# A decode step of attention beside a gated feed-forward layer: one section with its own semaphores, and a loop on TensorE

## The chip, the cores and the metric

The kernel runs on one core of a Trainium2 chip. The metric is the device time of one execution in microseconds. Three timed executions of the kernel before took 2523.05, 2523.11 and 2523.18 us; the median, 2523.11 us, is the time before. The engines are called as the profile calls them: PE is TensorE (PEld its weight loads), DVE is VectorE, ACT is ScalarE, POOL is GpSimd, and SP is SyncE, whose queue starts nearly all transfers. The data itself is moved by 16 DMA engines.

## What is computed

One token `x` of 512 values goes through two branches. Branch A is attention with 32 heads over a cache of 65,536 keys and values of 128 each; branch B is a gated feed-forward layer. A scalar gate mixes them.

```python
g = sigmoid((x * gate_w).sum(-1, keepdims=True))
q = (x @ wq)                                  # 32 heads of 128
scores = einsum("bhqd,bhkd->bhqk", q, k_cache) * (128 ** -0.5)
p = softmax(scores, axis=-1)
a = einsum("bhqk,bhkd->bhqd", p, v_cache) @ wo  # heads side by side
b = (silu(x @ w_gate) * (x @ w_up)) @ w_down
return g * a + (1 - g) * b
```

The two caches hold 32 x 65536 x 128 bf16 numbers each, 537 MB apiece. All else is small beside them.

## The kernel before

The caches are cut into N = 128 tiles. A tile is 128 keys on each of 128 partitions (NB = 128 keys of 128 numbers, 4 MB), and a head has G = 4 of them. Two tiles make a pair (8 MB), so there are M = 64 pairs, and two pairs to a head. The main loop (L424) is unrolled in Python and takes one pair a step. An even step (`first`) begins a head, an odd step ends it.

SBUF holds two K buffers of a pair each (`take`, `give`, the tiles `K_t`) and one V buffer of a pair (`V_buf`). In a step, DVE multiplies the K tile by the query in place (`products`, L261, 128x16384), halves the 128 products of each key to 16 by three additions in place (L265), and later reduces what TensorE made of them (`fold`, L289). TensorE adds the 16 columns of a key by four matmuls with the identity (`scores`, L274). After a head's last tile come the maximum (`row_max`), the exponentials on ACT (`exponentials`, L308) and their sum (`total`, `weight`). TensorE then multiplies the probabilities of the head before by its V tiles, 32 matmuls a tile (`values`, L330); with V two pairs behind K, step i works on V of pair i - 2. DVE takes the sums of a finished head out of PSUM (`head_copy`, L350 and L361), TensorE turns them into a column (`head_turn`, L367), ACT writes it to `oT` (L397), and at the end `project` (L406) multiplies all heads by `wo`.

The order of the work on each engine is written out by hand in that loop; the framework adds the semaphores. Two things in it matter here. In an odd step TensorE runs `values(2i-4)` ahead of `scores(2i)`; in an even step `scores(2i)` comes first. And the V loads are issued where their buffer comes free: after each half in an even step (`load_v(2i-2)`, `load_v(2i-1, 1)`, two transfers of 4 MB), after both halves in an odd step (`load_v(2i-2)`, one transfer of 8 MB). The K load of pair i + 2 (`load_k(i + 2)`) follows behind `scores(2i+1)`. SP issues all of these in this order, so that V of pair i - 1 and K of pair i + 2 alternate on its queue; both go through line 114. TensorE's program is the longest of all: every matmul of all 64 steps is in it once.

The feed-forward layer and the gate are worked into the first two steps, and the last pair of each cache and `wo` are loaded in smaller pieces at the end, into buffers that have come free.

Of the kernel before, what the change touches and what calls it, by code (L numbers as in the profile page):

```python
# [12 lines left out]

NB = 128
PAIR = 2 * NB
SLOTS = 2

QUAD = 4  # L20
# [5 lines left out]
V_CUTS = {3: (0, 64, NB), 2: (0, 64, NB), 1: (0, 32, 64, 96, 112, NB - TURNED, NB)}  # L26
EARLY = 16
LATE_CUTS = (EARLY, 24, 28, 30, 32)

GROUPED = 28  # L30


@with_exitstack
def kernel(
# [28 lines left out]
    assert Dh == P and G == 4 and NBH == 512 and H * D <= PAIR * Dh  # L63
    scale = float(Dh) ** -0.5

    consts = ctx.enter_context(tc.tile_pool(name="consts", bufs=1))
    ring = ctx.enter_context(tc.tile_pool(name="ring", bufs=1))
    small = ctx.enter_context(tc.tile_pool(name="small", bufs=2))
    psum_s = ctx.enter_context(tc.tile_pool(name="psum_s", bufs=2, space=bass.MemoryType.PSUM))
    psum_o = ctx.enter_context(tc.tile_pool(name="psum_o", bufs=2, space=bass.MemoryType.PSUM))  # L70
    psum_a = ctx.enter_context(tc.tile_pool(name="psum_a", bufs=1, space=bass.MemoryType.PSUM))
    psum_m = ctx.enter_context(tc.tile_pool(name="psum_m", bufs=2, space=bass.MemoryType.PSUM))

    ctx.enter_context(tc.manual_schedule())


    free = list(range(SLOTS))
    held = {}

    def take(name):  # L80
        slot = free.pop(0)
        held[name] = slot
        return ring.tile(
            [P, PAIR * Dh], bf16, name=name.split(".")[0], tag=f"slot{slot}"
        )

    def give(name):
        free.append(held.pop(name))


# [3 lines left out]
    consts.tile([P, 96], bf16, name="fill")  # L94
    xT = consts.tile([P, KT], bf16, name="xT")
    gwT = consts.tile([P, KT], bf16, name="gwT")
    with nc.allow_non_contiguous_dma(reason="small"):
        nc.scalar.dma_start(out=xT, in_=A_x[0, 0, :].rearrange("(p t) -> p t", t=KT))
        nc.scalar.dma_start(out=gwT, in_=gate_w.rearrange("(p t) -> p t", t=KT))

    nc.sync.dma_start(  # L101
        out=V_buf[:, : KT * H * Dh], in_=A_wq.rearrange("(p t) f -> p (t f)", t=KT)
    )
    wq_sb = V_buf[:, : KT * H * Dh].rearrange("p (t f) -> p t f", t=KT)

    K_tiles, V_tiles, S_tiles, F_tiles, P_tiles, O_tiles, q_tiles = {}, {}, {}, {}, {}, {}, {}


    def load(view, cache, m, cuts, start=0):
        h, g = divmod(m, MH)  # L110
        rows = cache[0, h, g * PAIR * P : (g + 1) * PAIR * P, :]
        src = rows.rearrange("(p j) d -> p j d", j=PAIR)
        for a, b in zip(cuts[:-1], cuts[1:]):
            nc.sync.dma_start(out=view[:, a:b, :], in_=src[:, start + a : start + b, :])

    def load_k(m):
        view = take(f"K_t.{m}").rearrange("p (j d) -> p j d", d=Dh)
        load(view, A_k_cache, m, (0, NB, PAIR) if m in (0, M - 1) else (0, PAIR))
        for i in range(2):
            K_tiles[2 * m + i] = view[:, i * NB : (i + 1) * NB, :]  # L120

    def load_v(n, half=0, spare=None):
        if n % G == 0 and spare is None:
            view = V_buf.rearrange("p (j d) -> p j d", d=Dh)
            V_tiles[n], V_tiles[n + 1] = view[:, :NB, :], view[:, NB:, :]
            load(view, A_v_cache, n // 2, (0, PAIR))
        else:
            view = V_buf if spare is None else spare
            view = view[:, half * NB * Dh : (half + 1) * NB * Dh]
            V_tiles[n] = view = view.rearrange("p (j d) -> p j d", d=Dh)  # L130
            load(view, A_v_cache, n // 2, V_CUTS.get(N - n, (0, NB)), n % 2 * NB)

    load_k(0)
    load_k(1)

    ident_f = consts.tile([P, P], f32, name="ident_f")
    make_identity(nc, ident_f[:])
    ident_b = consts.tile([P, P], bf16, name="ident_b")
    nc.scalar.activation(out=ident_b, in_=ident_f, func=ACT.Copy)
    ones_f = consts.tile([P, P], f32, name="ones_f")  # L140
    nc.vector.memset(ones_f, 1.0)

    ones_b = consts.tile([P, P], bf16, name="ones_b")
    nc.vector.memset(ones_b, 1.0)

    qT = consts.tile([P, H], f32, name="qT")
    rowsum = consts.tile([P, H], f32, name="rowsum")
    oT = consts.tile([P, H], bf16, name="oT")
    gval = consts.tile([P, 1], f32, name="gval")
    rg = consts.tile([P, H], f32, name="rg")  # L150
    HD = D // 2
    a_ps = [psum_a.tile([1, HD], f32, name=f"a{i}_ps") for i in range(2)]

    def queries():
        q_ps = psum_m.tile([P, H], f32, name="q_ps", tag="misc")
        for h in range(H):
            for t in range(KT):
                nc.tensor.matmul(
                    q_ps[:, h : h + 1],
                    lhsT=wq_sb[:, t, h * Dh : (h + 1) * Dh],  # L160
                    rhs=xT[:, t : t + 1],
                    start=(t == 0),
                    stop=(t == KT - 1),
                )
        nc.scalar.activation(out=qT, in_=q_ps, func=ACT.Copy)

    def query(h):
        diag = small.tile([P, P], bf16, name="q_diag")
        nc.scalar.activation(out=diag, in_=ident_f, func=ACT.Copy, scale=qT[:, h : h + 1])  # L169
        qb_ps = psum_m.tile([P, P], f32, name="qb_ps", tag="misc")  # L170
        nc.tensor.matmul(qb_ps, lhsT=ones_b, rhs=diag, start=True, stop=True)  # L171
        q_tiles[h] = small.tile([P, P], bf16, name="q_sb")
        nc.scalar.activation(out=q_tiles[h], in_=qb_ps, func=ACT.Copy)  # L173

    def load_wo(tile, cuts):
        t = tile[:, : H * D].rearrange("p (h n) -> p h n", n=D)
        runs = t.rearrange("p (g j) n -> p g (j n)", j=QUAD)
        rows = A_wo.rearrange("(h p) n -> p h n", p=P)
        row_runs = A_wo.rearrange("(g p j) n -> p g (j n)", p=P, j=QUAD)
        for a, b in zip(cuts[:-1], cuts[1:]):  # L180
            if b <= GROUPED:
                a, b = a // QUAD, b // QUAD
                nc.sync.dma_start(out=runs[:, a:b, :], in_=row_runs[:, a:b, :])
            else:
                nc.sync.dma_start(out=t[:, a:b, :], in_=rows[:, a:b, :])
        return t

    def feed_forward_in():
        gu_ps = psum_m.tile([P, 2 * FT], f32, name="gu_ps", tag="misc")
        for w in range(2):  # L190
            cols = wgu_sb[:, w].rearrange("p t (m c) -> p t c m", c=FT)
            for ft in range(FT):
                for t in range(KT):
                    nc.tensor.matmul(
                        gu_ps[:, w * FT + ft : w * FT + ft + 1],
                        lhsT=cols[:, t, ft, :],
                        rhs=xT[:, t : t + 1],
                        start=(t == 0),
                        stop=(t == KT - 1),
                    )  # L200
        gu_sb = consts.tile([P, 2 * FT], f32, name="gu_sb")
        nc.scalar.activation(out=gu_sb, in_=gu_ps, func=ACT.Copy)
        eg = consts.tile([P, FT], f32, name="eg")
        nc.scalar.activation(out=eg, in_=gu_sb[:, :FT], func=ACT.Exp, scale=-1.0)
        return gu_sb, eg

    def gate_sum():
        xg = consts.tile([P, KT], f32, name="xg")
        nc.vector.tensor_tensor(out=xg, in0=xT, in1=gwT, op=ALU.mult)
        xs = consts.tile([P, 1], f32, name="xs")  # L210
        nc.vector.tensor_reduce(out=xs, in_=xg, axis=AXIS.X, op=ALU.add)
        return xs

    def gate_exp(xs):
        g_ps = psum_m.tile([P, 1], f32, name="g_ps", tag="misc")
        nc.tensor.matmul(g_ps, lhsT=ones_f, rhs=xs, start=True, stop=True)
        eg2 = consts.tile([P, 1], f32, name="eg2")
        nc.scalar.activation(out=eg2, in_=g_ps, func=ACT.Exp, scale=-1.0)
        return eg2

    def gate_value(eg2):
        nc.vector.tensor_scalar_add(eg2, eg2, 1.0)
        nc.vector.reciprocal(gval, eg2)
        rest = consts.tile([1, 1], f32, name="rest")
        nc.vector.tensor_scalar(
            out=rest, in0=gval[0:1, :], scalar1=-1.0, scalar2=1.0, op0=ALU.mult, op1=ALU.add
        )
        return rest
# [41 lines left out]
    def scores(n):  # L270
# [11 lines left out]
        if n % 2:  # L282
            give(f"K_t.{n // 2}")
# [276 lines left out]
```

## Time and profile before

| What | Value |
|---|---|
| median of three timed executions | 2523.11 us |
| the profiled execution's own time | 2523.22 us |
| its span, first to last instruction | 2521.4 us |
| read from HBM | 1087.64 MB |
| busy: DVE / PE / PEld / ACT / POOL | 2260.4 / 1274.2 / 490.8 / 100.5 / 0.7 us |
| instructions on PE, as the trace records them | 5232 matmuls and 5232 weight loads |
| L261, product of a K tile | x128, 8685 ns each |
| L330, matmul of V | x4032, 409 ns recorded, 986.4 us together |
| L350 and L361, a head's sums | x31 each, 671 ns and 1020 ns |

A profile is one execution of the program, recorded instruction by instruction. Its span is a little shorter than its time, by 1.8 us here, which lie ahead of the first and behind the last recorded instruction. A group's "idle before" is the time its engine stood still just before its instructions, with the event that ended the wait. The chain of waits follows back from the last instruction to what released it, step by step. A queue's packets are what the DMA engines moved for it; the queue that is marked "instruction" brings the programs of the engines themselves.

### The profile page before, as it was taken

Reading aid. Unit: us, or ns where it says so; the run is one execution under the profiler, and the core shown is the slowest. Engines: PE = TensorE matmul, PEld = TensorE weight load, DVE = VectorE, ACT = ScalarE, POOL = GpSimd, SP = SyncE. Lnnn points to the kernel's source line nnn. Section 1 sums busy time; section 2 is a strip of 40 time slices with the busy share of each in tenths; the row PEclk is TensorE's granted clock in tenths of the full one; section 3 lists DMA queues with packets and bytes.
Section 4 is the critical chain, followed back from the end, with each engine's and each line's share of the span. In section 5 each row is a group of like instructions: output and inputs, shape, how many; then the busy total and the mean of one; then the engine's idle time right before and its main releaser. Section 6 shows DMA issues by size and latency. Waiting matters only on the chain.

```text
span 2521.4 us, 12044 instructions
## 1 busy us (share of the span) xinstructions
PE 1274.2 (51%) x5232; PEld 490.8 (19%) x5232; DVE 2260.4 (90%) x830; ACT 100.5 (4%) x317; POOL 0.7 (0%) x6
## 2 busy tenths in 40 slices
PE   3544654536535455444455453554545544446548
PEld 2211211212212122111122121221211211112213
DVE  5899999989999989899999898999998989999993
ACT  0000000000000000000000000000000000000000
POOL 0000000000000000000000000000000000000000
PEclk8767767767767677676777776776767767677779
DMA  9999999999999999999999999999999999999998
GB/s 415 436 434 433 436 435 430 436 434 433 433 430 436 435 432 432 435 433 442 432 433 432 430 435 434 437 432 433 432 436 432 435 437 429 437 432 432 433 432 374
DMA packets 26888, 1088.42 MB, mean 432 GB/s; under 512 B 3154, under 2 KB 3667, under 8 KB 4947
## 3 DMA queue, kind: packets, MB, share of 16 engines
q1 hardware_dynamic: 26546, 1087.65, 99.8%
q8 instruction: 41, 0.67, 0.1%
q14 instruction: 13, 0.10, 0.0%
q10 hardware_dynamic: 288, 0.00, 0.0%
HBM read 1087.64 MB, written 0.00 MB: 431 GB/s over the span
## 4 chain that ended last, share of the span: by engine, by line
DMA 51%; DVE 46%; PE 2%; issue 1%; another core or an unknown queue 0%; DVEq 0%; SPq 0%; ACT 0%
DMA K_t<-in_A_k_cache_dram 49%; DVE K_t L261 23%; DVE K_t L265 20%; PE S_ps L274 2%; DVE o_row L361 1%; DMA V_buf<-in_A_v_cache_dram 1%; DVE S_sb L289 1%; DVE O_sb L350 1%; DMA wo_late<-in_A_wo_dram 1%; PE O_ps L330 0%; DVE top L304 0%; PE a_ps L406 0%; DVEq L261 0%; SPq L101 0%
## 5 line engine op out<-in xcount | busy, mean ns | idle before, releaser
L261 DVE TENSOR_TENSOR K_t<-K_t,q_sb 128x16384 bf16<-128x16384 bf16 x128 | 1111.7, 8685 | 142.8 <-DMA K_t<-in_A_k_cache_dram 142.8
L330 PE MATMUL O_ps<-V_buf,P_sb 128*4 128x512 bf16 x4032 | 986.4, 409 | 361.4 <-DMA V_buf<-in_A_v_cache_dram 360.5
L265 DVE TENSOR_TENSOR K_t<-K_t 128x2048 bf16<-128x2048 bf16 (+1 forms) x372 | 996.0, 2677 | 8.3
L274 PE MATMUL S_ps<-K_t,ident_b 128*128 128x512 bf16 x576 | 208.3, 503 | 807.2 <-DVE K_t L265 806.8
L330 PEld LDWEIGHTS <-P_sb 128*4 128x4 bf16 x4094 | 364.9, 90 | 980.3 <-issue 534.3
L274 PEld LDWEIGHTS <-ident_b 128*128 128x128 bf16 x576 | 62.4, 113 | 899.4 <-issue 877.3
L289 DVE TENSOR_REDUCE S_sb<-S_ps 128x128 f32<-128x512 f32 x128 | 87.4, 683 | 65.9 <-PE S_ps L274 65.9
L397 ACT ACTIVATE oT<-oh_ps,rg 32x1 bf16<-32x1 f32 x112 | 28.6, 255 | 696.9 <-PE oh_ps L367 695.9
L299 PE MATMUL mT_ps<-diag,ones_f 128*128 128x128 f32 x64 | 24.8, 490 | 60.2 <-ACT diag L297 60.1
L173 ACT ACTIVATE q_sb<-qb_ps 128x128 bf16<-128x128 f32 x32 | 8.9, 278 | 911.6 <-PE qb_ps L171 911.6
L299 PEld LDWEIGHTS mT_ps<-diag,ones_f 128*128 128x128 f32 x64 | 15.6, 303 | 88.4 <-ACT diag L297 88.4
L361 DVE TENSOR_REDUCE o_row<-O_sb 4x128 f32<-4x512 f32 x31 | 31.6, 1020 | 1.1
L297 ACT ACTIVATE diag<-ident_f,m 128x128 f32<-128x128 f32 x32 | 12.8, 401 | 353.9 <-DVE m L295 353.9
L527 DVE CAST out_sb<-a_ps 1x256 bf16<-1x256 f32 x1 | 0.4, 412 | 27.2 <-PE a_ps L406 27.2
L308 ACT ACTIVATE P_sb<-S_sb,bias 128x512 bf16<-128x512 f32 x32 | 23.1, 722 | 1.0
L316 PEld LDWEIGHTS tot_ps<-rowsum,ones_f 128*128 128x128 f32 x64 | 20.7, 324 | 12.1 <-issue 9.2
L295 DVE TENSOR_REDUCE m<-S_sb 128x1 f32<-128x512 f32 x32 | 22.0, 686 | 1.1
L350 DVE TENSOR_TENSOR O_sb<-O_ps,ident_f 4x512 f32<-4x512 f32 x31 | 20.8, 671 | 1.5 <-PE O_ps L330 1.5
L306 ACT ACTIVATE bias<-top 128x1 f32<-128x1 f32 x32 | 6.5, 203 | 298.4 <-DVE top L304 298.4
L316 PE MATMUL tot_ps<-rowsum,ones_f 128*128 128x1 f32 x64 | 13.2, 276 | 0.0
L169 ACT ACTIVATE q_diag<-ident_f,qT 128x128 bf16<-128x128 f32 x32 | 12.8, 400 | 0.4
L321 DVE RECIPROCAL recip<-tot_ps 128x1 f32<-128x1 f32 x32 | 5.1, 161 | 7.8 <-PE tot_ps L316 7.8
(53 smaller groups left out, 115.5 us busy)
## 6 DMA issues: line engine op xcount, KB each, us to landing
V_buf<-in_A_v_cache_dram SPq DMA_DIRECT2D x62, 4096.0 KB, 22.5
K_t<-in_A_k_cache_dram SPq DMA_DIRECT2D x4, 4096.0 KB, 31.8
V_buf<-in_A_v_cache_dram SPq DMA_DIRECT2D x4, 2048.0 KB, 21.9
V_buf<-in_A_wq_dram SPq DMA_DIRECT2D x1, 4096.0 KB, 12.4
wo_early<-in_A_v_cache_dram SPq DMA_DIRECT2D x1, 4096.0 KB, 37.0
wo_late<-in_A_v_cache_dram SPq DMA_DIRECT2D x3, 1024.0 KB, 24.1
wo_early<-in_A_wo_dram SPq DMA_DIRECT2D x1, 2048.0 KB
V_buf<-in_B_w_gate_dram SPq DMA_DIRECT2D x1, 1792.0 KB, 54.6
```

Of the source, the lines that this page charges most:

```text
L261: yield nc.vector.tensor_tensor(out=K, in0=K, in1=q_rep, op=ALU.mult)
L265: yield nc.vector.tensor_tensor(out=K[:, :, 0:half], in0=K[:, :, 0:half], in1=K[:, :, half : 2 * half], op=ALU.add,)
L274: nc.tensor.matmul(S, lhsT=ident_b, rhs=K_tiles[n][:, :, c : c + QUAD], start=(c == 0), stop=(c == width - QUAD),)
L289: nc.vector.tensor_reduce(out=S_tiles[h][:, g * NB : (g + 1) * NB], in_=F_tiles.pop(n), axis=AXIS.X, op=ALU.add)
L295: nc.vector.tensor_reduce(out=m, in_=S_tiles[h], axis=AXIS.X, op=ALU.max)
L299: nc.tensor.matmul(mT_ps, lhsT=ones_f, rhs=diag, start=True, stop=True)
L308: nc.scalar.activation(out=P_tiles[h], in_=S_tiles[h], func=ACT.Exp, bias=bias, scale=scale, accum_out=rowsum[:, h : h + 1],)
L316: nc.tensor.matmul(tot_ps, lhsT=ones_f, rhs=rowsum[:, h : h + 1], start=True, stop=True)
L330: nc.tensor.matmul(O_tiles[h], lhsT=P_tiles[h][:, g * NB + j : g * NB + j + 4], rhs=V_tiles[n][:, j : j + 4, :], start=(g == 0 and j == 0) ...
L350: nc.vector.tensor_tensor(out=O_sb.rearrange("q (c d) -> q c d", c=4), in0=O.rearrange("q (c d) -> q c d", c=4), in1=diag, op=ALU.mult,)
L361: nc.vector.tensor_reduce(out=dst, in_=src, axis=AXIS.X, op=ALU.add)
L397: nc.scalar.activation(out=oT[part * A : (part + 1) * A, g * QUAD + j : g * QUAD + j + 1], in_=oh_ps[j * A : (j + 1) * A, :], func=ACT.Cop ...
```

## The change

The whole kernel is put into one section (`tc.tile_critical`), in which the framework adds no semaphores; the kernel counts its own (`Events`, `wait`). What each engine does is written out by itself: `vector_step`, `scalar_step`, `sync_step`, and on POOL `tell_of_v`. The arithmetic and the transfers are the same, but for these points.

- TensorE's work for the steps 2 to 62 is one loop body of 61 rounds (`pe.Fori`, `tensor_step`). As the body is the same in each round, all its addresses are fixed. Even and odd steps have one order: scores of the first tile, spread of the next query, sum, both V tiles, scores of the second tile, turn, maximum. A round waits on credits (`take`), semaphores that the others raise and that TensorE lowers again.
- DVE's last addition of a tile writes to a small tile of its own (`T_sb`), which TensorE reads for the scores.
- A head's sums are closed after each pair instead of after two pairs. ACT copies them out of PSUM (`o_copy`) and TensorE turns them, four small matmuls for each pair; ACT adds the two parts (`add_half_o`). DVE no longer does this (L350 and L361 go).
- The exponentials are done for each pair instead of for each head (256 columns, `P_sb` holds one pair), and DVE adds the two sums (`tsum`).
- POOL waits for each V landing and passes it on to TensorE as a credit (`tell_of_v`).
- At the end POOL waits for all and clears the semaphores.

The cut diff, with the lines taken out first:

```diff
-    mT_ps = tot_ps = None
-    for i in range(M - 1):
-        h, first = i // MH, i % MH == 0
...
-        if first:
-            scores(2 * i)
-        if mT_ps is not None:
-            tot_ps = total(h - 1)
-            mT_ps = None
-        if i >= 2:
-            values(2 * i - 4)
-            if first:
-                load_v(2 * i - 2)
-        if not first:
-            scores(2 * i)
...
-        vector = products(2 * i + 1)
-        next(vector)
-        fold(2 * i)
-        for _ in vector:
-            pass
...
-        scores(2 * i + 1)
-        if i == 0:
-            ff = feed_forward_in()
-        if i + 2 < M:
-            load_k(i + 2)
-        if not first:
-            fold(2 * i + 1)
-            mT_ps = row_max(h)
...
+    K_bufs = [ring.tile([P, PAIR * Dh], bf16, name=f"K{i}_buf") for i in range(2)]
+    V_buf = ring.tile([P, PAIR * Dh], bf16, name="V_buf")
...
+    T_sb = sb("T_sb", [P, NB, WIDTH], bf16)
...
+    P_sb = sb("P_sb", [P, PAIR], bf16)
...
+    S_ps = [psum.tile([P, NB, QUAD], f32, name=f"S{i}_ps") for i in range(2)]
+    O_ps = psum.tile([4, 4 * Dh], f32, name="O_ps")
...
+    c_S = [nc.alloc_semaphore(f"c_S{i}") for i in range(2)]
+    c_q, c_P, c_V, c_o, c_m = (nc.alloc_semaphore(n) for n in ("c_q", "c_P", "c_V", "c_o", "c_m"))
...
+    def load_v(i):
+        for n in (2 * i, 2 * i + 1):
+            wait(sync, pe_V, n - 1 if i % 2 else 2 * i)
+            if i % 2:
+                load_tile(V_half[n % 2], A_v_cache, n, (vA_in, vB_in)[n % 2])
+        if i % 2 == 0:
+            load_pair(V_buf, A_v_cache, i, vA_in)
+
...
+    def sync_step(m):
+        load_v(m - 1)
+        if m + 2 < M:
+            wait(sync, pe_S, 2 * m + 2)
+            load_k(m + 2)
...
+    def tell_of_v(i):
+        wait(pool, vA_in, 16 * (i + 1))
+        if i % 2 == 0:
+            pool.sem_inc(c_V, 2)
+        else:
+            pool.sem_inc(c_V, 1)
+            wait(pool, vB_in, 16 * ((i + 1) // 2))
+            pool.sem_inc(c_V, 1)
...
+    def add_halves(n, width, last, out=None):
+        K = K_half[n // 2 % 2][n % 2]
+        half, mark = Dh // 2, last
+        while half >= width:
+            wait(dve, dv, mark)
+            to = K[:, :, 0:half]
+            if half == width and out is not None:
+                wait(dve, pe_S, n)
+                to = out
+            ins = dve.tensor_tensor(out=to, in0=K[:, :, 0:half], in1=K[:, :, half : 2 * half], op=ALU.add)
+            if half == width and out is not None:
+                ins.then_inc(c_S[n % 2], 1)
+            else:
+                mark = dv(ins)
+            half //= 2
+        marks["K", n] = mark
...
+    def weight(h, t):
+        wait(dve, pe_t, t)
+        if h < H - 1:
+            wait(dve, dv, dv(dve.tensor_reduce(out=tsum[:, 0:1], in_=tot, axis=AXIS.X, op=ALU.add)))
+            total = tsum[:, 0:1]
+        else:
...
+    def vector_step(m):
+        h, b = divmod(m, MH)
+        width, to = (WIDTH, T_sb) if m < M - 1 else (LAST, None)
+        last = product(2 * m)
+        if b == 0:
+            top_of(h - 1)
+        else:
+            fold(2 * m - 1)
+        add_halves(2 * m, width, last, to)
+        last = product(2 * m + 1)
+        fold(2 * m)
+        if b == 1:
+            weight(h - 1, m - 1)
+        add_halves(2 * m + 1, width, last, to)
+        if b == 1:
+            row_max(h, fold(2 * m + 1))
...
+    def scalar_step(m):
+        h, b = divmod(m, MH)
+        if b == 0:
+            head_bias(h - 1)
+        wait(act, pe_V, 2 * (m - 2))
+        exponentials(h - 1, b, P_sb, PAIR).then_inc(c_P, 1)
+        if m == M - 1:
+            return
+        if b == 1:
+            query(h + 1, True)
+        else:
+            act.sem_inc(c_q, 1)
+        wait(act, pe_V, 2 * (m - 2) + 2)
+        o_copy(h - 1).then_inc(c_o, 1)
+        wait(act, pe_o, m - 1)
+        if b == 0:
+            marks["half_o"] = ac(copy(half_o[:, 0:1], oh))
+            act.sem_inc(c_m, 1)
+        else:
+            ac(head_out(h - 1, add_half_o()))
+            head_diag(h, True)
...
+    def take(credit):
+        pe.wait_ge(credit, 1)
+        pe.sem_inc(credit, -1)
...
+    def tensor_step():
+        take(c_S[0])
+        scores(0, T_sb, WIDTH)
+        take(c_q)
+        query_spread()
+        take(c_P)
+        total()
+        for i in range(2):
+            take(c_V)
+            pe_V(values(P_sb[:, i * NB : (i + 1) * NB], V_half[i], 0, NB, i == 0, i == 1))
+        take(c_S[1])
+        scores(1, T_sb, WIDTH)
+        take(c_o)
+        head_turn()
+        take(c_m)
+        max_turn()
...
+    with tc.tile_critical():
+        prologue()
+        for m in range(2, M):
+            vector_step(m)
+            scalar_step(m)
+            if m < M - 1:
+                sync_step(m)
+            tell_of_v(m - 2)
+        sync_end()
+        scalar_end()
+        vector_end()
+        sync_out()
+        with pe.Fori(0, M - 3):
+            tensor_step()
+        tensor_end()
+        for engine in (pe, act, dve):
+            engine.sem_inc(done.sem, 1)
+
+        pool.wait_ge(done.sem, 3)
+        pool.wait_ge(out_in.sem, 16)
+        pool.sem_clear(range(first_sem.num, last_sem.num + 1))
```

## The prediction

> **What bounds the kernel now.** I read the busy line first, then the packets of the queues.
>
> ```profile
> PE 1274.2 (51%) x5232; PEld 490.8 (19%) x5232; DVE 2260.4 (90%) x830; ACT 100.5 (4%) x317; POOL 0.7 (0%) x6
> q1 hardware_dynamic: 26546, 1087.65, 99.8%
> q8 instruction: 41, 0.67, 0.1%
> q14 instruction: 13, 0.10, 0.0%
> ```
>
> The data queue fills 99.8% of what 16 DMA engines have. In the trace a packet of 65,536 bytes takes 2.418 us, so 16 engines move 433.7 GB/s and 1087.65 MB need 2508 us. From the first packet (1.9 us) that ends at 2510. The last transfer of `wo` tells its landing by 16 marks, one of each engine: the first at 2510.2, the last at 2517.8 us. The fastest engine has no gap at all, the slowest is 7.6 us late, and the kernel ends with the slowest. What made it late stands in the chain of waits (start, length, what):
>
> ```profile
> 431.56 40.47 DMA K_t<-in_A_k_cache_dram
> 472.13 8.69 DVE K_t L261
> 508.82 41.73 DMA K_t<-in_A_k_cache_dram
> ...
> 974.18 41.93 DMA K_t<-in_A_k_cache_dram
> ...
> 1516.83 41.76 DMA K_t<-in_A_k_cache_dram
> ...
> 2059.46 41.72 DMA K_t<-in_A_k_cache_dram
> ```
>
> A K load takes 40.5 us with its queueing, and four take 1.3 us more, some 515 us apart. The 41 packets of q8 come 62 us apart, and 515 us is 8 to 9 of them. They are TensorE's program: 0.67 MB over 10,464 matmuls and weight loads is 64 bytes each, so one 16 KB packet brings 256 of them. In the marks of the K landings each such packet sets one engine back by 1.2 to 1.5 us (1.45 on average); nine engines take turns and are 5.9 to 7.6 us late at the end, five are not late at all.
>
> The third view is two steps of the timeline (start, length, engine, line):
>
> ```profile
> 1205.77 0.33 SPq L114 DMA_DIRECT2D V_buf<-in_A_v_cache_dram  x1
> 1207.33 0.33 SPq L114 DMA_DIRECT2D K_t<-in_A_k_cache_dram  x1
> 1209.34 8.69 DVE L261 TENSOR_TENSOR K_t<-K_t,q_sb 128x16384 bf16<-128x16384 bf16 x1 [2.85 <-DMA K_t<-in_A_k_cache_dram]
> ...
> 1218.88 9.80 PE L330 MATMUL O_ps<-V_buf,P_sb 128*4 128x512 bf16 x32 [11.58 <-DMA V_buf<-in_A_v_cache_dram]
> ...
> 1236.67 0.33 SPq L114 DMA_DIRECT2D V_buf<-in_A_v_cache_dram  x1
> ...
> 1247.91 8.69 DVE L261 TENSOR_TENSOR K_t<-K_t,q_sb 128x16384 bf16<-128x16384 bf16 x1 [0.87 <-DMA K_t<-in_A_k_cache_dram]
> ...
> 1264.77 1.86 PE L274 MATMUL S_ps<-K_t,ident_b 128*128 128x512 bf16 x4 [16.45 <-DVE K_t L265]
> ...
> 1267.16 14.77 PE L330 MATMUL O_ps<-V_buf,P_sb 128*4 128x512 bf16 x64 [0.30 <-DMA V_buf<-in_A_v_cache_dram]
> ```
>
> Each step starts when K lands and DVE waits for that (2.85 and 0.87 us): the transfers pace it. The odd step starts at 1209.3; its V tiles are multiplied as soon as they land, and the next V load is issued 27.3 us into the step. The even step does the scores first.
>
> **The change part by part.** *TensorE's program.* By the built order the loop body holds 73 bf16 matmuls (two instructions each), 6 in f32 (four each) and ten others: 180. Run straight, the program is some 1460 instructions, 6 packets instead of 41. If the loop is not fetched again, an engine is hit once by q8 instead of five times. What is left on the slowest: one packet (1.45 us), one or two of q14 (0.3 to 0.4 us each in the landing marks; ACT's program doubles, DVE's stays), and the 0.5 us spread of the first landings. That is about 2.2 us instead of 7.6: **-5.4 us** (bounds: -7.1, if only the spread stays; 0, if fetching stays).
>
> *The loop's back edge.* No loop is in this trace. Its price on TensorE lies between nothing and a fetch at each round; a stall there is covered, because after a round TensorE idles until DVE has added (16.45 us in the row at 1264.77). The packets are not covered; they are the first rival. I take none, as the nearest rows fetch a block once when it is entered first.
>
> *V released later in odd steps.* Scores now come first there as in the even step, so the even step's row holds: from K's landing 16.9 us to the scores, then 17.7 to the end of 64 matmuls (median over the even steps; 16.9 to 18.4). In the odd step DVE has a fold of 0.68 us in place of a maximum of 0.28, so scores start at 17.3. The query spread adds 0.3 (L171), the waits on credits 0.2 by estimate. V ends at 35.5, and SP has issued at 35.9 instead of 27.7. Queued behind that wait on SP is the K load; its own wait (scores of the second tile) ends at 36.6 anyway, 36.3 before. Ahead of both the DMA engines still move K, whose last mark comes 38.5 us after the landing before (1209.3 to 1247.8). The last data ends 0.3 us before its mark, and an issue needs 0.45 us to its first packet (output: 2519.68 to 2520.11). So the slowest engine has work until 38.2 and new work from 36.35: 1.9 us of room, cost **0**. Without it each microsecond too late costs 31 us, one for each odd step. Early engines that idle cost nothing, as they only wait for the slowest.
>
> *POOL between V's landing and TensorE.* One semaphore hop more, 0.03 us (V's last matmul to SP's issue) to 0.4 (the longest hop in the barrier). In even steps V lands at 19.3 and is now wanted at 19.6: **0**, at most 0.1 of the 1.9.
>
> *DVE.* It loses L350 and L361 (1.7 us a head) and gains one tiny reduction (0.16, as L211). It waited for K already: **0**. `T_sb` is an addition of the same form.
>
> *ACT and turning.* For each pair a copy (0.59, L344), two or five small copies (0.26 each), 8 turning matmuls (1.0 us together, L380). ACT is at 4%, and TensorE does this while it waits for DVE. In an odd step the maximum now stands behind them on ACT, some 2 us later, and DVE asks for it 8.7 us into the next step: **0**.
>
> *Start and end.* One more hop before the first issue (0 to 0.7, the first barrier's wait; I take 0.3), and at the end POOL's wait, clearing and another round of drains (0 to 1.5; barrier hops there take 0.4 to 0.7; I take 0.8): **+1.1**.
>
> Sum against the profiled execution: 2523.2 (2521.4 of span and 1.8 around) - 5.4 + 1.1 = 2518.9. The median of the runs is 0.1 below the profiled one, which is no difference here. I forecast **2519 us**, -0.16%; its own range is 2517 to 2521.
>
> **The rivals.** *The loop is fetched again in each round.* The profile shows that entering a block fetches the next one. Packet k starts when 256k less some 70 instructions are recorded, so the program starts 70 into a block and the loop lies at 739 to 918, over the edge at 768: each round crosses it. If that drops the block in which the loop begins, a round costs one to three packets. At 61 rounds, 1.45 us and nine engines each is 9.8 us: 2528.7, 2538.5 or 2548. Two are likeliest, the block of the loop's head and the one past its end: **2538.5**, slower. From one packet a round on it loses to the gain. For it: every block entry in this trace fetched. Against: no row shows a block dropped.
>
> [...]
>
> *V comes too late.* If TensorE issued V at its slow pace throughout (0.43 us a weight load, as the first 13 of the odd step; 27.3 us for 64), SP would issue at 48.4 and the engines would stand for 10.5 us: 31 x 10.5 gives 2844. A smaller slip, weight loads of 90 ns no longer overlapped, adds 5.8 and leaves 3.9 us: 2640. Against both: 64 matmuls take 14.8 us in every even step.
>
> *The ends cost nothing and q14 stays away from the slowest engine:* 2517.
>
> **How the numbers follow.** Forecast 0.48; fetched again 0.35 (one packet a round 0.07, two 0.18, three 0.10); V late 0.09; cheaper ends 0.08. A run tells 0.2% from no change, 5 us here: below 2518.1 is faster, above 2528.2 slower. Faster: the cheap ends and 0.14 of the forecast's 0.48 (its lower end), 0.22. Same: the rest of the forecast, 0.34, and half of one packet a round, 0.04. Slower: what is left, 0.40. The range is 2516.5 to 2540: the forecast, the cheap ends, one packet and most of two, about 0.8.
>
> **What would show it.** q8's packets: some 6 if the forecast holds, 60 and more for the first rival. The last `wo` marks: spread of 2 to 3 us, the last near 2513. K legs of the chain without the 1.3 us steps every 515 us. In odd steps the V issue 36 us behind K's landing, and the data queue at 99% or more; a share of 99.3% or less, or V issues later than 38, would be the second rival. A span that falls while the chain's DMA legs do not would prove the whole reading wrong.

## The result, and the profile after

The changed kernel took 2539.78 us (median of four timed executions, 2537.21 to 2541.26); the kernel before took 2523.14 us beside it. The ratio is 1.0063, 95% interval [1.0046, 1.0081]: slower by 16.6 us, where 2519 was forecast. The profiled execution took 2539.18 us, its span is 2537.4 us.

First the busy line and the queues, from the page of the changed kernel (queue: packets, MB, share of the 16 engines' span):

```profile
PE 1334.6 (53%) x5813; PEld 557.8 (22%) x5813; DVE 2217.8 (87%) x802; ACT 187.8 (7%) x503; POOL 0.7 (0%) x6
q1 hardware_dynamic: 26546, 1087.65, 99.6%
q8 instruction: 5, 0.08, 0.0%
q14 instruction: 14, 0.11, 0.0%
```

TensorE's program is fetched in 5 packets where it took 41: the loop is not fetched again. The share of the data queue has fallen by only 0.2 points, but the span has grown by 16 us, so there is something in the 99.6% that moves no data. It lies in the odd steps. The same stretch of the timeline as before, an odd step's end and the two steps behind it (start, length, engine, line):

```profile
1253.41 0.33 SPq L174 DMA_DIRECT2D V_buf<-in_A_v_cache_dram  x1
...
1254.72 0.33 SPq L174 DMA_DIRECT2D K_buf<-in_A_k_cache_dram  x1
...
1257.45 8.69 DVE L264 TENSOR_TENSOR K_buf<-K_buf,q_sb 128x16384 bf16<-128x16384 bf16 x1 [1.31 <-DMA K_buf<-in_A_k_cache_dram]
...
1284.61 7.24 SPq L178 DMA_DIRECT2D V_buf<-in_A_v_cache_dram  x2
...
1296.12 8.69 DVE L264 TENSOR_TENSOR K_buf<-K_buf,q_sb 128x16384 bf16<-128x16384 bf16 x1 [4.74 <-DMA K_buf<-in_A_k_cache_dram]
...
1313.47 1.87 PE L446 MATMUL S_ps<-T_sb,ident_b 128*128 128x512 bf16 x4 [19.06 <-PEq L442]
...
1315.69 15.66 PE L467 MATMUL O_ps<-V_buf,P_sb 128*4 128x512 bf16 x64
...
1331.38 0.33 SPq L174 DMA_DIRECT2D V_buf<-in_A_v_cache_dram  x1
```

K of the second step shown lands at 1296.1, its scores start 17.4 us later, its V values 19.6, and V is released and issued again at 1331.4, 35.3 us into the step: the path is the predicted one to half a microsecond. The first of the even step's two halves is issued much earlier (at 1284.6, for a landing of K at 1296.1). How close the odd step's issue is to the end of what the engines have to do is seen in the transfer's own time. These are the rows of the issues (how many transfers of 8 MB, median us from issue to landing), first of the kernel before, then of the changed one:

```profile
V_buf<-in_A_v_cache_dram SPq DMA_DIRECT2D x31, 31.0
```

```profile
V_buf<-in_A_v_cache_dram SPq DMA_DIRECT2D x31, 23.9
```

8.39 MB take 19.3 us at 433.7 GB/s. Before, the load stood 11.7 us in the queue behind other work; now it stands 4.6, and that with the last engines counted. By the landing marks, the K transfer ahead of it ends on the first engine a median of 1.1 us after the end of the V issue (0.39 at the least), against 6.9 us before. This distance is called the lead below. From the start of the issue at 1253.41 to V's first packet go 0.96 us, 0.63 of them behind the issue's end. Fourteen of the 16 engines stood dry (without a packet to move) for 0.1 to 0.4 us there, and the first packet of each took about 3.0 us in place of 2.418.

Over the run 669 packets of 64 KB take longer than 2.45 us, 202 us together too long, or 12.7 us on each engine; before there were 39, with 19 us. The gaps around the odd steps' V issues add some 5 us on each engine. Not every odd step pays: from the second on, 14 of the 30 have a lead under 1 us and lose 0.86 us on each engine in the mean, in gaps and slow packets together; the four with a lead above 2.5 us lose 0.11. The steps that hold the late V grow from 1154.5 to 1171.0 us in all (30 of them), the others stay (1126.6 and 1124.4); between pair 3 and pair 62 the run loses 13.6 us, and behind it 2.0.

### The profile page after: what moved, and what is told of

Same layout as the page of the kernel before. It is cut to its first block, busy times and chain, and to the rows that moved or that the text cites. A ratio compares the mean times of both kernels' runs of the same rounds, so it can differ in the third digit from the quotient of the medians.

```text
span 2537.4 us, 14083 instructions
## 1 busy us (share of the span) xinstructions
PE 1334.6 (53%) x5813; PEld 557.8 (22%) x5813; DVE 2217.8 (87%) x802; ACT 187.8 (7%) x503; POOL 0.7 (0%) x6
## 3 DMA queue, kind: packets, MB, share of 16 engines
q1 hardware_dynamic: 26546, 1087.65, 99.6%
## 5 line engine op out<-in xcount | busy, mean ns | idle before, releaser
L264 DVE TENSOR_TENSOR K_buf<-K_buf,q_sb 128x16384 bf16<-128x16384 bf16 x128 | 1112.1, 8688 | 214.0 <-DMA K_buf<-in_A_k_cache_dram 214.0
L275 DVE TENSOR_TENSOR K_buf<-K_buf 128x8192 bf16<-128x8192 bf16 x252 | 849.5, 3371 | 4.3
L446 PE MATMUL S_ps<-T_sb,ident_b 128*128 128x512 bf16 x488 | 180.0, 505 | 1033.9 <-PEq L442 1033.6
L467 PEld LDWEIGHTS O_ps<-V_buf,P_sb 128*4 128x4 bf16 x3968 | 349.9, 89 | 603.0 <-issue 159.5
L446 PEld LDWEIGHTS S_ps<-T_sb,ident_b 128*128 128x128 bf16 x488 | 44.9, 110 | 1123.7 <-issue 1107.5
L333 ACT ACTIVATE O_sb<-O_ps 4x512 f32<-4x512 f32 x63 | 63.5, 1008 | 1290.3 <-PE O_ps L467 1290.3
L275 DVE TENSOR_TENSOR T_sb<-K_buf 128x2048 bf16<-128x2048 bf16 x122 | 149.4, 1224 | 4.2
L475 PE MATMUL oh_ps<-ident_f,O_sb 4*128 4x1 f32 x504 | 64.6, 245 | 9.0 <-PEq L442 8.2
L475 PEld LDWEIGHTS oh_ps<-ident_f,O_sb 4*128 4x128 f32 x504 | 60.7, 186 | 38.6 <-issue 38.2
L463 PEld LDWEIGHTS tot_ps<-rs,ones_f 128*128 128x128 f32 x126 | 34.1, 330 | 18.0 <-issue 17.9
L329 DVE CAST out_sb<-a_ps 1x256 bf16<-1x256 f32 x1 | 0.4, 413 | 27.2 <-PE a_ps L484 27.2
```

Of the source, the lines that this page charges most:

```text
L264: return dv(dve.tensor_tensor(out=K, in0=K, in1=q_rep, op=ALU.mult))
L275: ins = dve.tensor_tensor(out=to, in0=K[:, :, 0:half], in1=K[:, :, half : 2 * half], op=ALU.add)
L329: dv(dve.tensor_copy(out=out_sb[:, :HD], in_=a_ps[0]))
L333: return act.activation(out=out, in_=in_, func=ACT.Copy, scale=scale)
L446: ins = pe.matmul(S_ps[n % 2], lhsT=ident_b, rhs=src[:, :, c : c + QUAD], start=(c == 0), stop=(c == width - QUAD),)
L463: pe_t(pe.matmul(tot[:, :n], lhsT=ones_f, rhs=rs[:, :n], start=True, stop=True))
```

## The experiments

Two theories stood at the start. *Late V*: the odd step's V load is issued so late that the engines run dry. *The loop*: something else that the loop costs (its back edge, its fetches) takes the 16 us.

**V in halves in every step.** The first half is then released 7 us earlier (POOL's `tell_of_v` is changed with it, to pass on the second half in every step):

```diff
 def load_v(i):
     for n in (2 * i, 2 * i + 1):
-        wait(sync, pe_V, n - 1 if i % 2 else 2 * i)
-        if i % 2:
-            load_tile(V_half[n % 2], A_v_cache, n, (vA_in, vB_in)[n % 2])
-    if i % 2 == 0:
-        load_pair(V_buf, A_v_cache, i, vA_in)
+        wait(sync, pe_V, n - 1)
+        load_tile(V_half[n % 2], A_v_cache, n, (vA_in, vB_in)[n % 2])
```

> The changed kernel, but V is loaded in two transfers of 4 MB in odd steps too, each issued when its own half of the V buffer is free. Late-V theory (the 16 us were lost because the one 8 MB V transfer of an odd step is issued about 35 us after K's landing, when most DMA engines have run dry or are about to): the first half is now issued about 27 us after K's landing, 11 us before the engines run dry, and the time falls to 2519 us (2517 to 2521), which is the sum of the prediction. Loop theory (the loop's rounds, the credits or POOL's relay slow the stream, wherever V is issued): it stays within 3 us of 2540.

Measured: 2525.49 us (2524.18 to 2526.04), ratio 1.0006 [0.9997, 1.0015]. Long 64 KB packets fall from 669 to 4. That count holds K alone here, as V now goes in packets of 32 KB; of these 43 take longer than 1.23 us, where 221 did in the changed kernel and 35 before. 14.3 of the 16.6 us are back with the loop untouched; but 2519 is not reached.

**The same, with the 61 rounds written out:**

```diff
-        with pe.Fori(0, M - 3):
+        for _ in range(M - 3):
             tensor_step()
```

> As the run before, with the 61 rounds written out one after the other in TensorE's program instead of looped; all else alike. Fetch theory (each 16 KB of program costs one DMA engine 1.45 us, nine in turn): about 45 packets on the queue for TensorE's program, the last marks of wo spread over 7 to 8 us, and 5 us more than the looped form (2523 to 2525). If the packets were hidden, the two forms would agree within 1 us.

Measured: 2528.18 us (2527.74 to 2529.58), ratio 1.0021 [1.0012, 1.003]; 47 packets of q8 in place of 5, and the last marks of `wo` lie 8.1 us apart in place of 6.3:

```profile
q8 instruction: 47, 0.77, 0.1%
```

So the loop does save, but 2.7 us by the medians (3.6 by the means of the eleven executions of each) and not 5. The 5.4 of the forecast was too much here.

**Scores first in the kernel before**, and nothing else of the change:

```diff
+        if not first:
+            scores(2 * i)
         ...
-        if not first:
-            scores(2 * i)
```

(the first pair goes ahead of `values(2i-4)`, the second was behind it.)

> The kernel before, with one thing of the change alone: in odd steps the scores of the first tile stand ahead of the first V tile on TensorE, so that V's buffer comes free some 8 us later. No loop, the framework's semaphores, the same transfers. Late-V theory: the time rises by 12 to 25 us (2535 to 2548), V issues in odd steps 34 to 36 us after K's landing. Loop theory: within 2 us of 2523.

Measured: 2536.48 us (2533.64 to 2539.59), ratio 1.0048 [1.0033, 1.0064]. Its issue row is that of the changed kernel, and its data queue too:

```profile
q1 hardware_dynamic: 26546, 1087.65, 99.6%
q8 instruction: 41, 0.67, 0.1%
V_buf<-in_A_v_cache_dram SPq DMA_DIRECT2D x31, 23.9
```

With 41 packets of q8, no loop, no own semaphores, the order alone costs 13 us (the four executions spread over 6 us). The lead of V is 1.3 us in the median.

**V later still in the changed kernel:**

```diff
     def sync_step(m):
+        if m % 2:
+            wait(sync, pe_S, 2 * m + 2)
         load_v(m - 1)
```

> The changed kernel, with V's transfer in odd steps held back until the second tile's scores are done too, about 1.2 us later. Late-V theory: all engines are now dry when it comes, each of 31 odd steps loses about 1.2 us more, 30 to 40 us in all (2570 to 2580). Loop theory: no change, 2537 to 2542.

Measured: 2576.51 us, one execution. The median lead falls from 1.1 to -0.1 us: by then the first engine is out of work before the issue has ended. 1.2 us in each of 31 odd steps is 37 us, and 36.7 came.

**Two steps in the loop.** This puts the order of the odd step back and keeps the loop, the loads, and all else:

```diff
-    def tensor_step():
-        take(c_S[0])
-        scores(0, T_sb, WIDTH)
+    def tensor_step(odd=False):
+        if not odd:
+            take(c_S[0])
+            scores(0, T_sb, WIDTH)
...
             pe_V(values(P_sb[:, i * NB : (i + 1) * NB], V_half[i], 0, NB, i == 0, i == 1))
+            if odd and i == 0:
+                take(c_S[0])
+                scores(0, T_sb, WIDTH)
...
-        with pe.Fori(0, M - 3):
+        with pe.Fori(0, (M - 3) // 2):
             tensor_step()
+            tensor_step(True)
+        tensor_step()
```

> The changed kernel, loads and all, but the loop of TensorE holds two steps (30 rounds and one step behind them): in the odd step the values of the first V tile come ahead of the first scores again, the others follow as before, so that V is released some 27 us into the step instead of 35. Late V: the odd step's V issue is 6 us or more ahead of the next landing (after: 1.1), packets longer than 2.45 us fall from 669 to under 150, the last two pairs start 16 us earlier than in the changed kernel, and the time falls to 2518 to 2525: below the run with halves (2525.5), as packets of 64 KB come back, and above 2519 by what TensorE's own end chain takes, which was 2.5 us longer than before in the run with halves. If the two-step body (about 360 instructions, over at least one edge of 256) is fetched again in each round, the instruction queue of TensorE shows 40 to 100 packets instead of 5, and the time stays at 2530 or above. If late V is not what counts, 2538 to 2541.

Measured: 2523.01 us (2522.83 to 2524.62), ratio 0.9999 [0.999, 1.0008]. The step of the profile that answers to the one above (its K lands at 1284.9), and the rows of the page:

```profile
1284.86 8.69 DVE L264 TENSOR_TENSOR K_buf<-K_buf,q_sb 128x16384 bf16<-128x16384 bf16 x1 [4.72 <-DMA K_buf<-in_A_k_cache_dram]
...
1294.69 9.27 PE L467 MATMUL O_ps<-V_buf,P_sb 128*4 128x512 bf16 x32 [9.73 <-PEq L442]
...
1303.89 1.09 PE L446 MATMUL S_ps<-T_sb,ident_b 128*128 128x512 bf16 x4
1304.91 7.07 PE L467 MATMUL O_ps<-V_buf,P_sb 128*4 128x512 bf16 x32
...
1312.01 0.33 SPq L174 DMA_DIRECT2D V_buf<-in_A_v_cache_dram  x1
```

```profile
q8 instruction: 7, 0.11, 0.0%
q14 instruction: 14, 0.11, 0.0%
V_buf<-in_A_v_cache_dram SPq DMA_DIRECT2D x31, 30.9
```

The V issue is 27.2 us into the step again, the load stands in the queue as long as before (30.9), the long packets fall from 669 to 13, the lead is 8.0 us, and the 16.8 us against the changed kernel are gone. The run with halves and the run with V later still leave TensorE's order as it is in the changed kernel, so it is not the order apart from V. Late V is the whole of the loss. What is left open by it is the gain: q8 has 7 packets in place of 41 and the time is that of the kernel before. The end of both runs, from the traces:

```text
us                               before   two steps   two steps, tail moved
first mark of the last wo load  2510.20     2510.48     2510.34
last mark of it                 2517.79     2516.47     2516.43
output issued                   2519.35     2518.81     2518.05
span                            2521.4      2521.2      2520.5
```

The transfers end 1.3 us earlier, not 5.4: 15 engines are within 3 us of the first, and one is 6.0 us behind. Behind the last mark the new kernel takes 0.8 us more to its output and 0.35 more from there.

**The tail.** In the chain of waits of the run with halves, TensorE's last work, not the transfers, sets the end:

```profile
2476.11 3.51 PE S_ps L443 x8
...
2486.57 7.00 PE O_ps L464 x32
...
2495.72 20.30 PE O_ps L464 x94
```

From 2476 to the output the chain holds TensorE's work, with short steps of DVE and ACT between. Before, eight such scores took 1.89 us there, after a wait of 1.75 us; here 3.5, after a wait of 2.5. The granted clock goes with it: from 2476 to 2480 it is 0.57 here and 1.00 in the kernel before. In all eleven profiles the last eight scores took 1.9 us after waits of up to 1.75 us, and 2.75 to 3.5 us after waits of 1.97 us and more. The last column of the table is a run with two moves:

```diff
-        if b == 1:
+        if b == 1 and m < M - 1:
             weight(h - 1, m - 1)
         ...
             row_max(h, fold(2 * m + 1))
+        if m == M - 1:
+            weight(h - 1, m - 1)
...
-        values(lower, V_half[1], 0, NB // 2, False, False)
+        values(lower, V_half[1], 0, 3 * NB // 4, False, False)
         scores_direct(N - 1, LAST)
-        values(lower, V_half[1], NB // 2, 3 * NB // 4, False, False)
+        pe_V(values(lower, V_half[1], 3 * NB // 4, NB, False, True))
         wait(pe, ac, marks["diag", H - 1])
         max_turn()
-        pe_V(values(lower, V_half[1], 3 * NB // 4, NB, False, True))
```

> As the run with two steps in the loop, with two small moves behind the loop: DVE's three small operations of the last weight come behind the last maximum instead of ahead of the last additions (0.5 us), and the third quarter of a V tile's values comes ahead of the last scores, so that TensorE does not stand 2.5 us there and then takes its matmuls at 0.43 us each (3.5 instead of 1.9 us for eight). If TensorE's chain from the last scores on sets the end once the transfers are on time, this gains 2 to 2.6 us against the run without it (to 2517 to 2522). If the transfers set the end, the two runs are equal within 0.5 us.

Measured: 2522.27 us (2522.06 to 2522.66), ratio 0.9995 [0.9986, 1.0004]: 0.7 us less than without, between the two expectations. In the run without it the scores already took 1.9 us, so most of the expected gain was not there to be had; the move brought TensorE's chain 1.1 us forward, and then the transfers are last again:

```profile
2484.59 29.26 DMA K_buf<-in_A_wo_dram
2513.85 0.04 issue
2513.89 3.67 PE a_ps L486 x32
```

It is the best of all runs. Its eleven executions all lie below the 21 of the kernel before beside it (2523.18 to 2524.80), but the interval of the ratio holds 1: a gain of some 1 us is likely and not shown.

**Which engine is late, and why.** The trace does not say on which engine a packet ran. I strung the packets into 16 rows, so that each begins where another ended. In the run with two steps one 64 KB packet takes about 2.95 us near 168, 553, 941, 1328, 1665 and 2043 us, and at each of these times there is an 8 KB packet of q14; at 2427 the same happens to a 32 KB packet (1.74 us in place of 1.213). From 941 on the last mark of the K landings falls back by some 0.9 us at each of them, while the second-latest goes from 1.9 to 3.0 us in all. This would be DVE's program, if all of it went through one engine: by estimate, at the 64 bytes that an instruction of TensorE takes (0.67 MB over 10,464), a packet of 8 KB holds 128 instructions, some ten steps. The test makes DVE's program longer, by increments of an unused semaphore:

```diff
+    def filler(count):
+        for _ in range(count):
+            dve.sem_inc(fill_sem, 1)
...
         last = product(2 * m)
+        filler(6)
...
         last = product(2 * m + 1)
+        filler(6)
```

> The run with two steps in the loop, with 12 increments of an unused semaphore added to DVE's program in each step (some 740 instructions; about 125 more in DVE's ten steps between two of its program fetches would double it). Theory: the one engine that was 6.0 us behind the others at the last transfer was made late by the seven fetches of DVE's program, which all land on the same engine, 0.95 us each. Then that engine alone becomes late, in steps twice as often as every 385 us, the queue of the other engines' programs shows 20 to 22 packets instead of 14, the marks of the last transfer lie 11 to 13 us apart instead of 6.0, 14 of the 16 engines stay within 3 us, and the last mark comes 4.5 to 6.5 us later; the time grows by 4 to 6 us, to 2527 to 2529. Rival: the lateness of that engine comes from something else (its rows of the cache, its own packets): the spread stays at 6 to 7 us and the time within 1 us of 2523.0. The increments themselves cost DVE less than the 2 us it waits in each step.

Measured: 2529.39 us (2528.58 to 2532.0), ratio to the kernel before 1.0023 [1.0013, 1.0033], 6.4 us over the run without the filling. The profiled execution is the longest of the ten, 2532.0 us.

```profile
q8 instruction: 7, 0.11, 0.0%
q14 instruction: 19, 0.16, 0.0%
```

The three latest of the 16 marks of K landings, in us behind the first of the landing, about every 460 us:

```text
K landing near     two steps          with filling
  432            1.7  1.9  2.0      1.6  1.8  3.4
  896            1.9  1.9  1.9      1.6  1.8  5.1
 1360            1.8  1.9  3.6      1.7  1.8  7.7
 1823            1.9  2.4  4.3      0.8  0.8  7.5
 2287            1.9  3.0  5.2      2.5  2.5  8.1
```

One engine alone falls back, by 0.9 us each 195 us in place of each 385. That settles the cause: DVE's program, and one engine. The added instructions did not delay the loads in another way: the V issue still comes 27.0 us into the odd step. The size at the end was missed: the marks lie 7.1 us apart and not 11 to 13, with 19 packets of q14 where 20 to 22 were expected. What fits the figures is that from about 8 us on (7.5 to 8.1 in the last three rows) the late engine holds up the whole: the next load is issued when K has landed on the slowest and the work of a step is done, and by then the others have less left to move (the lead of the even step's first half falls from 7.2 to 3.4 us in the median, to 0.3 at the least). The first mark of the last `wo` load is 6.3 us later, the last 7.3; the rest of the 9.0 us between the two profiled executions lies behind it, where the last eight scores took 3.3 us again.

**How much of a loop TensorE keeps.** The run with halves, with four and with twelve steps in the body (shown for twelve; with four it is `Fori(0, 15)` and `range(4)`):

```diff
-        with pe.Fori(0, M - 3):
-            tensor_step()
+        with pe.Fori(0, 5):
+            for _ in range(12):
+                tensor_step()
+        for _ in range(1):
+            tensor_step()
```

> The run with halves, with four steps in TensorE's loop body (716 instructions of 64 bytes, 46 KB, over two or three edges of 256) and 15 rounds plus one step. If TensorE keeps only two blocks of its program, as the fetched-again rival has it, each round fetches three to four: 45 to 60 packets on its instruction queue, a time as the unrolled run's (2528). If it keeps as much as has run without being fetched so far and more, 8 to 12 packets and a time as the run with halves (2525.5).

> The same with twelve steps in the body (2148 instructions, 137 KB) and five rounds plus one step. Kept whole: some 15 packets. [...] Time 2525 to 2529.

Measured, one execution each: 2524.19 us with 8 packets of q8 (four steps), 2529.62 us with 58 (twelve).

```profile
q8 instruction: 8, 0.13, 0.0%
```

```profile
q8 instruction: 58, 0.95, 0.1%
```

46 KB are kept through 15 rounds; 137 KB are not kept whole (some 15 packets were expected for that), and in five rounds more is fetched than the program written out takes (58 packets against 47). With 50 packets more the execution took 5.4 us more. Where between 46 and 137 KB the keeping ends, no run shows.

## Why the prediction was wrong

- ***V released later in odd steps*: this step failed, and with it the sign.** Its path was right: 35.5 us to the end of V's values was predicted, and the issue came at 34.8 and 35.3. What failed is its price: "1.9 us of room, cost 0" and "Early engines that idle cost nothing, as they only wait for the slowest". The room is the lag of the slowest engine, and that is a stock, not an income. In an odd step with a short lead, as the one shown, the early engines lose up to 0.4 us dry and some 0.6 us on a slow first packet, and fall back towards the slowest; the next odd step takes from what is left. The leads of the first odd steps of the changed kernel are 5.7, 2.4, 1.9 and 0.8 us. From there on the lead swings: it falls by about 0.5 us a step, from some 2.6 to under 1, and goes back up (what sets it back is not shown). The marks lie 1.2 to 3.1 us apart all the while, so no group of engines is left that could wait without cost. A smaller part: from the issue's end to the first packet it took 0.63 us, where 0.45 was taken from the small output transfer. Measured: 16.8 us (the run with two steps against the changed kernel), 13 with the order alone in the kernel before.
- *V comes too late*, the second rival, was the right mechanism (engines that stand without work) with the wrong threshold and the wrong cause, as TensorE was not slow. It asked for an issue later than 38 us or a share of 99.3% or less. At 35 us and 99.6% it had already begun. The price that the prediction gave for a slip beyond the room, 31 us for each microsecond, held: 36.7 us for 1.2, in one execution.
- *The loop is fetched again* was wrong, though its 2538.5 us lies near the result. q8 shows 5 packets, and the loop crosses the edge that the rival asked for (a packet at 112.6 us falls into its first round; the next comes at 2489.6, behind the loop). That the result lies by its figure is luck. With 46 KB in the body there were 8 packets; only at 137 KB were there more (58) than with the rounds written out (47).
- *TensorE's program*, -5.4 us: fetches fell as predicted, the term was mis-sized. With V on time the last mark came 1.3 us earlier, and the loop alone saved 2.7 us in the pair of runs with halves. The step left "one or two of q14 (0.3 to 0.4 us each)" on the slowest engine. It has seven, all of DVE's program, at 0.9 us each, and that engine is about as late without TensorE's program (6.0 us) as nine others were with it (6.1 to 7.6 by the last marks of `wo` in the kernel before).
- *Start and end*, +1.1: measured 0.8 behind the last mark and 0.35 behind the output's issue, 1.1 in all, in the run with two steps. The sum agrees, in part by luck, as the place was another: not only the barrier but TensorE's own chain, which the forecast did not look at. In the kernel before the two were already level: TensorE was done with all else at 2515.20 us, and the piece of `wo` that it needed next landed at 2515.22. By these two figures an earlier end of the transfers alone would have gained little; it takes both.
- *POOL*, *DVE*, *ACT and turning*, *the back edge*: nothing was seen that they cost, though no run tries them one by one. In the run with two steps the whole change moves the time by 0.4 us.
- Not settled: why the run with halves stays 2.5 us above the run with two steps. It moves 30,866 packets where the other moves 26,546 (4 MB loads go in 32 KB packets, two of 1.213 us for one of 2.418), its first mark of the last load is 1.2 us later, and its last eight scores took 1.6 us longer, at the lower clock (0.57). The scores go far to explain it: the run with four steps in the body has the same loads and 1.9 us for these scores, and took 2524.19 us. It is one execution, so the shares stay open. A loop for DVE, to lower its fetches as those of TensorE's program fell (41 packets to 5), was not tried.

## What to carry to other kernels

When transfers bound the kernel, cost a later issue by the lead it leaves ahead of the *first* engine to finish, not the last: in this kernel the lag between engines covered a stall once and was used up (leads of 5.7, 2.4, 1.9 and 0.8 us in the first odd steps), while the stall came back. Here a lead above 2.5 us cost 0.11 us on each engine and one under 1 us cost 0.86, in the mean of four and of 14 steps. When removing one source of lateness, ask which engine is the next latest and what makes it late, before the whole of the lag is booked as gain. One body for two kinds of steps is an order change for one of them; a body of both kept the order here and cost two packets (7 in place of 5).

## What the runs showed of the hardware

- TensorE kept a loop over an edge of 256 instructions through 61 rounds (5 packets), and a body of 46 KB through 15 (8 packets), but not one of 137 KB (58 packets, 47 with the rounds written out).
- One DMA engine fell back with DVE's program, by 0.9 us per 8 KB packet (every 385 us, and every 195 us with the filling), while TensorE's 41 packets left nine engines 6.1 to 7.6 us late in the kernel before.
- In the step shown, the 14 DMA engines that had run dry took some 3.0 us each for their first 64 KB packet in place of 2.418. At leads of 1.5 to 2.1 us some first packets were slow with hardly a gap before them: at the V issue of 782.5 us, with a lead of 2.1, four took 3.0 to 3.9 us behind gaps of at most 0.1 us.
- The last eight scores took 1.9 us at a granted clock of 1.00 and 3.5 us at 0.57, the latter behind a wait of 2.5 us.
